# Linear attention into an RWKV channel mix: the attention output handed over by DMA transposes instead of TensorE transposes

## Chip, cores, metric

One core of one Trainium2 chip. The metric is the device time of one execution in microseconds (us). Kernels that are compared were run in turn on the same chip, in several rounds. A run over 1.5% above the fastest of the same kernel counts as slow, and ratios use fast runs alone.

## The reference

Eight batches, 8 heads, 576 tokens, head width 64. Linear attention makes features of q and k (exp of a projection, with its largest magnitude taken off, and exp of the negative), and its output, 576 x 512 per batch, is the input of a channel mix:

```python
proj = x @ w_phi; proj = proj - max(abs(proj)); phi = concat(exp(proj), exp(-proj))
kv = phi(k).T @ v;  z = sum(phi(k));  attn = (phi(q) @ kv) / (phi(q) @ z + 1e-6)
x = attn, heads side by side                       # (8, 576, 512)
xk = mu_k * x + (1 - mu_k) * x_prev                # x_prev: the token before, 0 for the first
xr = mu_r * x + (1 - mu_r) * x_prev
k = relu(xk @ w_k);  v = (k * k) @ w_v;  r = sigmoid(xr @ w_r)
out = r * v
```

## The kernel before

Work goes by pairs of heads, 32 in all (4 per batch). A token is p*9 + s, and the nine values of s are called slots. Attention leaves `x_sc` with tokens on the partitions; the channel mix needs `xs` with features on the partitions. That hand-over is what the change touches. Every instruction group is an `op` with an engine and a planned duration; a long list, `ORDER`, gives the order in which they are emitted, and each engine is given its own in that order.

```python
def rd():                      # VectorE: normalise, out of PSUM
    s["rd"] = small.tile([128, 2, 5], FP, name="rden")
    ...
    nc.vector.tensor_tensor(s["x"]..., ndv[:, :, :, 0:64], s["rd"].to_broadcast(...), op=ALU.mult)

def xt():                      # TensorE: five 128x128 transposes into PSUM
    ps = motile(("mo", "x" + N), "ps_x")
    ...
    for G in range(5):
        nc.tensor.transpose(px[:, G * 128:128 + G * 128],
                            s["x"][:, 2 * G:2 * G + 2, :].rearrange("p h d -> p (h d)"), ident)

def xe():                      # VectorE: four copies PSUM -> xs
    nc.vector.tensor_copy(xs[:, a, 128:640]..., s["px"][:, 0:512]...)
    nc.vector.tensor_copy(xs[:, a, 1:64], s["px"][:, 448:511])       # the slot shifted by one token
    for hh in range(2):
        r = slice(64 * hh, 64 * hh + 64)
        nc.vector.tensor_copy(xs[r, a, 64:128], s["px"][r, 512 + 64 * hh:576 + 64 * hh])

def df():                      # VectorE: x - x_prev
    nc.vector.tensor_tensor(s["d"], xs[:, a, 64:64 + S], xs[:, a, 0:S], op=ALU.subtract)
# then mix(0), mix(1): xk and xr, and h, r, v: the products of the channel mix
```

SyncE's queue issues the output stores (72) and, for batches 2 to 7, one large DMA transpose of q and k each. GpSimd issues the loads of q, k and v, which cast from float32 to bf16.

## Time and profile before

| | before |
|---|---|
| median of the runs | 319.1 us (318.1 to 319.9) |
| TensorE busy / VectorE busy | 283.8 / 251.9 us of a span of 317.5 |
| mean granted TensorE clock | 0.988 |
| VectorE's wait for the transposes of the hand-over | 3.3 us in all |

In profile lines PE is TensorE (PEld its weight loads), DVE VectorE, ACT ScalarE, POOL GpSimd, and a q after a name is that engine's queue; a bracket at a line's end is the engine's idle time before it and what ended it. Busy time is the union of an engine's instructions; the span less that is its idle time (33.7 us on TensorE). The clock is the share of full speed that TensorE was granted.

### The profile page before, as it was taken

The page shows a single profiled execution, that of the slowest core. Times are in us where ns is not written, and L with a number is a line of the kernel's source. Part 1 is how long each engine was busy: PE and PEld are TensorE (multiplying, and loading weights), DVE is VectorE, ACT ScalarE, POOL GpSimd, SP SyncE. Part 2 cuts the span into 40 slices and gives each one's busy share as a digit, 9 for nine tenths or more (in the row PEclk, how much of TensorE's full clock was granted, in tenths as well). Part 3 has the DMA queues.
Part 4 walks back from the last instruction along what each step waited for, and adds up shares of the span by engine and source line. Part 5 has one row for each costly group of instructions (what it writes and reads, how often), then busy time and mean ns, then how long its engine had stood idle before and what let it go on. Part 6 is the DMA issues. An engine that isn't in the chain of part 4 may idle for free.

```text
span 317.5 us, 9126 instructions
## 1 busy us (share of the span) xinstructions
PE 283.8 (89%) x3830; PEld 164.1 (52%) x3830; DVE 251.9 (79%) x466; ACT 216.6 (68%) x318; POOL 145.0 (46%) x248
## 2 busy tenths in 40 slices
PE   1676786988999998999999999999999999999993
PEld 1464464545555654555555654555555655554541
DVE  4656999889989899998987997998887987683021
ACT  2468797667768875787688865779769578733610
POOL 8636311575375465455344632465624504603710
PEclk9999979899999999999999999999999999999999
DMA  8999996087399699574039930367052022114134
GB/s 149 203 209 205 209 162 70 0 129 134 74 186 208 126 168 232 100 139 88 0 68 154 238 53 18 55 145 144 2 125 46 2 46 60 30 39 95 34 68 99
DMA packets 49769, 34.25 MB, mean 108 GB/s; under 512 B 30656, under 2 KB 44352, under 8 KB 49728
## 3 DMA queue, kind: packets, MB, share of 16 engines
q0 software_dynamic: 14624, 16.48, 32.3%
q1 hardware_dynamic: 34960, 16.89, 26.2%
q8 instruction: 30, 0.49, 0.6%
q10 hardware_dynamic: 144, 0.29, 0.3%
q14 instruction: 11, 0.09, 0.1%
HBM read 33.62 MB, written 9.44 MB: 136 GB/s over the span
## 4 chain that ended last, share of the span: by engine, by line
PE 67%; DVE 21%; issue 3%; ACT 3%; DMA 2%; POOL 2%; SPq 0%; DVEq 0%; ACTq 0%
PE ps_v L747 15%; PE ps_h L714 15%; PE ps_r L733 7%; PE ps_nd L607 4%; DVE nm L514 4%; PE ps_kv L588 3%; DVE nm L519 3%; PE ps_x L631 3%; DVE xk L652 2%; PE ps_k L502 2%; PE ps_k L552 2%; DVE x_sc L621 2%; PE ps_ve L832 2%; PE ps_q L502 2%; PE ps_qT L560 2%
## 5 line engine op out<-in xcount | busy, mean ns | idle before, releaser
L725 POOL TENSOR_TENSOR kk<-krelu 128x512 bf16<-128x512 bf16 x64 | 67.0, 1058 | 60.1 <-ACT krelu L720 59.9
L529 ACT ACTIVATE k<-ps_k 128x1024 bf16<-128x1024 f32 x64 | 62.8, 1032 | 9.0 <-PE ps_k L552 8.7
L573 ACT ACTIVATE q<-ps_qT 128x1024 bf16<-128x1024 f32 x64 | 62.7, 1031 | 7.2 <-PE ps_qT L566 7.1
L714 PE MATMUL ps_h<-xk,wk_bf 128*128 128x512 bf16 x256 | 63.6, 381 | 1.2 <-DVE mT L547 0.6
L720 ACT ACTIVATE krelu<-ps_h 128x512 bf16<-128x512 f32 x64 | 38.5, 603 | 34.6 <-PE ps_h L714 28.3
L747 PE MATMUL ps_v<-wv_bf,kk 128*128 128x512 bf16 x256 | 59.7, 379 | 0.0
L514 DVE TENSOR_REDUCE nm<-ps_k 128x8 f32<-128x1024 f32 x32 | 39.0, 1220 | 5.1 <-PE ps_k L502 4.7
L519 DVE TENSOR_REDUCE nm<-ps_q 128x8 f32<-128x1024 f32 x32 | 38.9, 1218 | 3.1 <-PE ps_q L502 2.9
L753 DVE SCALAR_TENSOR_TENSOR ob<-rt,ps_v 128x512 f32<-128x512 bf16 x32 | 21.9, 685 | 22.3 <-PE ps_v L747 20.1
L747 PEld LDWEIGHTS <-kk 128*128 128x128 bf16 x256 | 23.9, 98 | 26.3 <-issue 0.7
L714 PEld LDWEIGHTS <-wk_bf 128*128 128x128 bf16 x256 | 23.2, 98 | 27.1 <-issue 3.5
L538 POOL CAST mhl<-nm 128x16 bf16<-128x16 f32 x32 | 7.4, 230 | 64.0 <-DVE nm L514 58.2
L733 PE MATMUL ps_r<-wr_bf,xr 128*128 128x512 bf16 x128 | 32.6, 380 | 0.1
L652 DVE SCALAR_TENSOR_TENSOR xk<-diff,mu_k_t,xs 128x576 bf16<-128x576 bf16 x32 | 30.4, 951 | 0.4
L739 ACT ACTIVATE rt<-ps_r 128x512 bf16<-128x512 f32 x32 | 19.2, 604 | 15.9 <-PE ps_r L733 15.9
L652 DVE SCALAR_TENSOR_TENSOR xr<-diff,mu_r_t,xs 128x576 bf16<-128x576 bf16 x32 | 28.9, 903 | 0.1
L621 DVE TENSOR_TENSOR x_sc<-ps_nd,rden 128x640 bf16<-128x640 f32 x32 | 26.4, 825 | 1.1
L502 PEld LDWEIGHTS <-qkT 64*128 64x128 bf16 x512 | 17.7, 97 | 13.3 <-issue 10.2
L607 PEld LDWEIGHTS <-q 128*128 128x128 bf16 x512 | 20.6, 101 | 6.2 <-issue 2.0
L607 PE MATMUL ps_nd<-kv,q 128*128 128x65 bf16 x512 | 22.7, 198 | 0.9 <-DVE qkT L298 0.7
L588 PE MATMUL ps_kv<-v,k 64*128 64x65 bf16 x1024 | 22.5, 192 | 0.6 <-DVE x_sc L621 0.2
L523 POOL COPY v<-vt 128x576 bf16<-128x576 bf16 x32 | 22.9, 737 | 0.0
(82 smaller groups left out, 433.3 us busy)
## 6 DMA issues: line engine op xcount, KB each, us to landing
out_dram<-ob SPq DMA_DIRECT2D x72, 128.0 KB, 2.4
nat<-in_k_dram POOLq DMA_DIRECT2D x6, 576.0 KB, 10.9
nat<-in_q_dram POOLq DMA_DIRECT2D x6, 576.0 KB, 9.7
vt<-in_v_dram POOLq DMA_DIRECT2D x6, 576.0 KB, 9.8
wk_bf<-in_moe_w_k_dram POOLq DMA_DIRECT2D x1, 1024.0 KB, 12.4
wv_bf<-in_moe_w_v_dram POOLq DMA_DIRECT2D x1, 1024.0 KB, 10.0
nat<-in_k_dram POOLq DMA_DIRECT2D x3, 288.0 KB, 8.5
nat<-in_q_dram POOLq DMA_DIRECT2D x3, 288.0 KB, 8.7
```

Source lines behind the costliest of these rows:

```text
L514: nc.vector.tensor_reduce(s["nm"][:, 0, :], s["k"].rearrange("p a (g f) -> p (a g) f", f=128), axis=AX.X, op=ALU.max, apply_absolute_value ...
L519: nc.vector.tensor_reduce(s["nm"][:, 1, :], s["q"].rearrange("p a (g f) -> p (a g) f", f=128), axis=AX.X, op=ALU.max, apply_absolute_value ...
L529: nc.scalar.activation(s[f"k{pn}"], s["k"].rearrange("p a (g f) -> p (a g) f", f=128), AF.Exp, scale=(1.0 if pn == 0 else -1.0))
L573: nc.scalar.activation(t.rearrange("f h (c p) -> f c h p", c=8), s["qT"].rearrange("f a (g h p) -> f (a g) h p", g=4, h=2), AF.Exp, scale= ...
L607: nc.tensor.matmul(ps[:, bk, o * 65:(o + 1) * 65], lhsT=s[f"q{pn}"][:, h, G * 128:(G + 1) * 128], rhs=s["kv"][:, h, pn, :], start=(o == 0 ...
L621: nc.vector.tensor_tensor(s["x"].rearrange("p (b s) d -> p b s d", b=2), ndv[:, :, :, 0:64], s["rd"].to_broadcast([128, 2, 5, 64]), op=ALU ...
L652: nc.vector.scalar_tensor_tensor(out=t[:, a, (b % 2) * S:(b % 2 + 1) * S], in0=s["d"], scalar=mu[:, a:a + 1], in1=xs[:, a, 0:S], op0=ALU.m ...
L714: nc.tensor.matmul(ps, lhsT=wk_bf[:, c, fc * 128:(fc + 1) * 128], rhs=xkt[bp][:, c, m0:m0 + 512], start=(c == 0), stop=(c == NDC - 1))
L720: nc.scalar.activation(s["kr", fc], s[fc], AF.Relu)
L725: nc.gpsimd.tensor_tensor(s["kk"][:, fc, :], s["kr", fc], s["kr", fc], op=ALU.mult)
L733: nc.tensor.matmul(ps, lhsT=xrt[bp][:, c, m0 + ci * 128:m0 + (ci + 1) * 128], rhs=wr_bf[:, c, :], start=(c == 0), stop=(c == NDC - 1))
L747: nc.tensor.matmul(ps, lhsT=s["kk"][:, fc, ci * 128:(ci + 1) * 128], rhs=wv_bf[:, fc, :], start=(fc == 0), stop=(fc == NFC - 1))
```

## The change

The intent: TensorE and VectorE are the two full engines, so take the transposes off the first and the copies out of PSUM (the memory where TensorE leaves its products) off the second, and let the DMA write `xs` directly. Side parts: the q0 tail is computed per head (so that both heads' tails land in the same rows), the factor 0.5 on w_v goes into relu as a scale of 0.5**0.5, the output slots are stored in another sequence, the large transpose is cut in two, the load of w_phi goes to ScalarE's queue, and `ORDER` was searched anew for all this. The core of the diff (the order and small lines cut):

```diff
+            x2 = s["x"].rearrange("p h d -> p (h d)")
+            for o, r, c0, c1 in ((64, 128, 0, 256), (320, 64, 512, 640), (384, 128, 256, 512)):
+                nb = (c1 - c0) // 128
+                nc.sync.dma_start_transpose(out=xs[:, a, o:o + nb * r].rearrange("p (g t) -> p g t", g=nb),
+                                            in_=x2[0:r, c0:c1])
+        def xu():
+            nc.vector.tensor_copy(xs[:, a, 1:64], xs[:, a, 576:639])
         def df():
-            nc.vector.tensor_tensor(s["d"], xs[:, a, 64:64 + S], xs[:, a, 0:S], op=ALU.subtract)
+            nc.vector.tensor_tensor(s["d"][:, 0:320], xs[:, a, 320:640], xs[:, a, 0:320], op=ALU.subtract)
+            nc.vector.tensor_tensor(s["d"][:, 320:576], xs[:, a, 64:320], xs[:, a, 320:576], op=ALU.subtract)
...
-            for pn in range(2):
-                nc.tensor.matmul(ps[:, 1, 195:325]..., lhsT=(tqp, tqn)[pn][b][:, a, :], rhs=s["kv"][:, :, pn, :], ...)
+            for h in range(2):
+                for pn in range(2):
+                    nc.tensor.matmul(ps[:, 1, 195 + 65 * h:260 + 65 * h],
+                                     lhsT=(tqp, tqn)[pn][b][:, a, 64 * h:64 * h + 128], ...)
...
-        op("xt" + N, "PE", 0.38, ...)
-        op("xe" + N, "DVE", 0.97, ...)
+        op("xz" + N, "SP", 1.0, ("xt", n), xz, ["rd" + N], ...)
+        op("xz" + N + ".d", "DMA", 2.2, ("xt", n), None, ["xz" + N], rel=[("x", n)])
+        op("xu" + N, "DVE", 0.1, ("xe", n), xu, ["xz" + N + ".d"])
...
-                nc.scalar.activation(s["kr", fc], s[fc], AF.Relu)
+                nc.scalar.activation(s["kr", fc], s[fc], AF.Relu, scale=HALF)
```

The planned costs in the `op` lines: 1.0 us on SyncE's queue for all three transposes of a pair, and 2.2 us to land.

## The prediction

> **What bounds the kernel now.** I read the page first (busy shares, the slices, the chain that ended last), then busy time by stretch, then the timeline of one attention pair's hand-over to the channel mix, then the groups, then the queue of SyncE.
>
> The busy shares and the row of slices:
>
> ```profile
> PE 283.8 (89%) x3830; PEld 164.1 (52%) x3830; DVE 251.9 (79%) x466; ACT 216.6 (68%) x318; POOL 145.0 (46%) x248
> ...
> PE   1676786988999998999999999999999999999993
> ...
> PE 67%; DVE 21%; issue 3%; ACT 3%; DMA 2%; POOL 2%; SPq 0%; DVEq 0%; ACTq 0%
> ```
>
> A slice is 317.5/40 = 7.9 us. TensorE is nearly full from the ninth slice (64 us) to the end; before that it is not. The last line is the chain that ended last: two thirds TensorE, a fifth VectorE, nothing else of weight. The same by stretch (us, then busy us of PE, PEld, DVE, ACT, POOL, clock, DMA share, GB/s):
>
> ```profile
> 0.00:64.00 64.00, 43.53 (x711) 29.93 (x713) 49.57 (x102) 42.31 (x65) 29.55 (x69) 0.95 0.89 150
> 64.00:280.00 216.00, 208.09 (x2952) 119.06 (x2947) 190.86 (x346) 163.66 (x237) 105.25 (x170) 1.00 0.55 102
> 280.00:317.50 37.50, 32.19 (x181) 15.12 (x177) 11.44 (x20) 10.58 (x18) 10.23 (x10) 0.99 0.33 71
> ```
>
> From 64 to 280 us TensorE is busy 208.1 of 216 us (96%) and VectorE 190.9 (88%): TensorE bounds, VectorE is close behind, and with both this full each sometimes makes the other wait. Before 64 us loads (DMA share 0.89) and VectorE hold TensorE to 68%. After 280 us only channel-mix products are left and no pair. So what the change saves must be saved in the first two stretches.
>
> One hand-over in the timeline (start us, duration us):
>
> ```profile
> 159.43 0.45 PE L631 MATMUL ps_x<-ident,x_sc 128*128 128x128 bf16 x5
> 159.67 1.45 PEld L747 LDWEIGHTS <-kk 128*128 128x128 bf16 x8
> 159.72 1.89 PE L747 MATMUL ps_v<-wv_bf,kk 128*128 128x512 bf16 x8
> 159.92 0.42 DVE L637 COPY xs<-ps_x 128x512 bf16<-128x512 bf16 x1 [1.15 <-PE ps_x L631]
> 160.26 0.18 DVE L639 COPY xs<-ps_x 128x63 bf16<-128x63 bf16 x1
> 160.36 0.38 DVE L642 COPY xs<-ps_x 64x64 bf16<-64x64 bf16 x2
> 160.78 0.46 DVE L646 TENSOR_TENSOR diff<-xs 128x576 bf16<-128x576 bf16 x1
> 161.27 0.82 DVE L652 SCALAR_TENSOR_TENSOR xk<-diff,mu_k_t,xs 128x576 bf16<-128x576 bf16 x1
> ```
>
> Durations overlap on an engine, so I count from start to start: the five transposes hold TensorE 159.72-159.43 = 0.29 us (not the 0.45 shown), the four copies hold VectorE 160.78-159.92 = 0.86 us, the difference 0.49 us.
>
> **What the Trainium skill says.**
> - "VectorE: DVE Perf Modes", section "The three transpose paths", gives 390 ns for a 128x128 transpose on TensorE and 1309 ns through the DMA. Here TensorE's transpose takes 219 ns alone and 0.29/5 = 0.06 us in a run, so a DMA transpose is no faster thing; its merit is only that it occupies neither bound engine and needs no copy out of PSUM.
> - "DMA: Bandwidth & Descriptors", section "DMA Transpose (X-bar)", demands a 2-byte type, a partition count that is a multiple of 16, SBUF as destination, and one stream of transposes at a time. The new transposes are bf16 on 128 or 64 partitions, and all go out on SyncE's queue beside the old ones: allowed.
> - The same page, section "Anatomy of one DMA", puts a fixed cost of about 2 us on a DMA for completion. It is written for GpSimd's path; the trace shows 2.4 us to landing for an output store issued from SyncE, which agrees in size.
> - "VectorE: DVE Perf Modes", section "Rules for kernel authors", says bf16 from SBUF to SBUF runs tensor_tensor at twice the plain rate. The trace agrees: the difference takes 458 ns (median), while the scaled add of the same 576 elements takes 819.
>
> **The change, part by part.**
>
> Transposes off TensorE: 32 pairs x 0.29 = -9.3 us of TensorE's queue. The chain gives line 631 3% of the span, 0.03 x 317.5 = 9.5 us, the same size.
>
> Copies off VectorE: 32 x 0.86 = -27.5 us. What comes back: the shifted slot is copied alone (63 columns; the like copy above starts 0.10 us before its follower) and the difference is cut into 320 and 256 columns. The cut adds one fixed share. I take it from the two scaled adds, which start 0.73 us apart elsewhere in this trace, less 576 columns at 0.96 per ns (the skill's VectorE clock, "Trainium Kernel Development and Optimization", NeuronCore Architecture) = 0.60: 0.13 us. So +32 x 0.23 = +7.4 us.
>
> Half into relu: the 1.22 us scaling of wv_bf goes, and relu gets a constant scale, free on the same instruction: -1.2 us of VectorE once.
>
> q0 tails per head: two products of 130 columns become four of 65. In the timeline 16 products of 65 columns run 0.51 us from start to start, 0.032 each, so four take 0.13 us, against 0.11 for the two: +0.02 x 32 = +0.6 us. Four more small fills at the start (88 ns for a like one): +0.4 us of VectorE, under the loads.
>
> Sum: TensorE 283.8-9.3+0.6 = about 275 us busy; VectorE 251.9-27.5+7.4-1.2+0.4 = about 231 us.
>
> DMA and SyncE: a pair issues three DMA transposes, 4.5 blocks of 128x128. The old transpose carries 36 blocks, 5.50 us of issue and 9.0 us to landing, so 0.153 us a block, and 3.5 us from the end of issue to landing. 4.5 blocks give 0.7 us by size; a small store takes 0.6 us to issue, so three instructions could take 1.8. I take 1.3 us of issue, 32 x 1.3 = 42 us in all, on a queue that mostly waits. To landing: 1.3 + 2.4 to 3.5 = 4 to 5 us after x_sc is ready. Before, TensorE and VectorE did it in 0.29 + 0.86 plus a short wait. So a pair gets 2 to 4 us more latency. That is hidden where the order puts other VectorE work between.
>
> I added up, from the new order and this trace's start-to-start times, the VectorE work between each pair's normalisation and its first reader of the landed data: 1.9 to 10.4 us, median about 4.9. With 4.5 us needed, 13 pairs of 32 have less, and are short by 14 us in all. But VectorE has waits of its own in that time (it will be idle about a quarter of the span), and a stall of VectorE reaches TensorE only in part: I charge a quarter, about 3.5 us.
>
> The gain on the path: TensorE -9.3 +0.6 = -8.7 us; VectorE is freed by 21 us, and its 21% of the chain suggests some 0.21 x 21 = 4.4 us; then +3.5 for late landings. -8.7 -4.4 +3.5 = -9.6 us. 319.8 - 9.6 = 310.2, and I round down to **309.5 us**, as the order was searched again for the lighter engines.
>
> **The rivals.**
> 1. *The wait for the landing takes the place of the copies.* Loads fill the DMA in the first 50 us, and an input load of 576 KB takes about 10 us to land; transposes share its engines. If landing takes 6.5 us, the same sum of shortfalls is 54 us, VectorE (in order) holds back the reductions behind it, and a quarter of that is 13 us: 319 to 322 us. For it: the old transposes landed in 7.3 to 11.6 us. Against: they are eight times as large, and DMA is only half busy after 64 us.
> 2. *SyncE's queue blocks.* Its waits in order are long; who waited for whom on it (total us, times, longest us):
>
> ```profile
> SPq L760 <- DVE ob L753: 124.9, 16, 18.6
> SPq L305 <- DMA nat<-in_k_dram: 56.0, 2, 34.5
> ```
>
> A transpose behind such a wait would be late. Against: I compared the new order, and no pair's transposes stand behind a store whose result VectorE makes after that pair's x_sc; the large transposes are cut in two (2.8 us each), and few stand in between. If it did happen for a third of the pairs: 316 us.
> 3. *Nothing much moves*, because the freed engine time is not where the end is set (the first 64 us are held by loads; the last 37 us contain no pair): 314 to 317 us. Against: 28 or so of the 32 hand-overs lie in the full stretch.
> 4. *More than the removed work comes back.* TensorE is idle 8 us between 64 and 280 and 20 us before; a VectorE with 21 us less to do could close a third of that: 300 to 303 us.
>
> **Range and chances.** Centre 309.5. Rival 4 sets the low end, 301; rivals 1 to 3 the high end, 318. Two per cent is 6.4 us, so faster means under 313.4. My central sum clears that by 4 us; rivals 1, 2 and 3 together have about three chances in ten. Faster 0.71, within 0.23, slower 0.06.
>
> **What would show it.** Right: the group of ps_x gone; TensorE near 275 and VectorE near 231 us; three transposes of x_sc per pair, 1 to 1.8 us of issue and 2.4 to 4 us to landing; VectorE's waits for the DMA of xs under 15 us in total; the stretch from 64 us on still full of TensorE. Wrong: if VectorE waits for xs by more than 30 us and TensorE has holes there, rival 1; if SyncE's transposes wait at the queue's head behind stores, rival 2; if TensorE's busy time falls by 9 but its idle time grows by as much without waits on xs, the order found elsewhere gave it back.

## More of the kernel before

The profile's own lines stand in the prediction. One more is needed later, from who waited for whom (total us, times, longest):

```profile
DVE xs L637 <- PE ps_x L631: 3.3, 5, 1.2
```

VectorE's first copy (line 637) waited five times for TensorE's transposes, never long.

## The result and the profile after

The changed kernel takes 354.5 us (median of 4 runs, 351.1 to 357.3) against 319.1 us. The ratio is 1.103, with a 95% interval of 1.097 to 1.108: slower by 10%. (A ratio is the mean time of one kernel's fast runs over that of the other's of the same rounds, so not quite the ratio of the quoted medians.) The profiled run was one of the slower, 357.3 us with a span of 355.5; a second profile is reported below and reads the same.

The page's busy shares, the slices, and the chain that ended last:

```profile
PE 283.7 (80%) x3690; PEld 163.3 (46%) x3734; DVE 230.7 (65%) x405; ACT 215.7 (61%) x318; POOL 143.0 (40%) x248
...
PE   1877486869836999956993999899729998987994
...
PEclk9998668999969999997897899999968999999999
...
PE 40%; DVE 20%; DMA 16%; SPq 12%; issue 4%; POOL 4%; ACT 2%; DVEq 0%; ACTq 0%; POOLq 0%
DMA xs<-x_sc 13%; SPq L646 9%; PE ps_v L761 8%; PE ps_h L728 8%; PE ps_r L747 4%; PE ps_kv L599 3%; PE ps_nd L618 2%; DVE xk L661 2%; DVE nm L525 2%; SPq L313 2%; DVE nm L530 2%; DVE xr L661 2%; DVE x_sc L634 2%; PE ps_he L815 2%; DVE ob L767 2%
```

VectorE's busy time fell by 21 us to 230.7, as planned. TensorE's did not fall, although nine microseconds of transposes are gone, and its row now has holes all along. The clock's row has holes at nearly the same places. The chain that ended last now runs through the new transposes: 13% of the span in their landing and 9% in their issue (line 646), 22% of 355.5 = 78 us where there was nothing. TensorE's idle time is 355.5 - 283.7 = 71.8 us, 38 more than before, which is the whole difference of the spans (355.5 - 317.5 = 38). (44 of TensorE's 3734 matmuls are missing from this profile; the second profile has all, with 285.9 us busy of a span of 354.3.)

Who waited for whom, and the instructions on the tile x_sc with the time from issue to landing of its transposes (durations in ns, minimum/median/maximum):

```profile
DVE xs L650 <- DMA xs<-x_sc: 44.5, 15, 9.9
```

```profile
L646 SPq DMA_TRANSPOSE xs<-x_sc x96: 1167/1240/3963, 30.2 to 322.3; - x96
...
DMA to landing us min/median/max: 2.3/3.3/10.4
```

VectorE's first reader of the landed data waits 44.5 us in all, in 15 of the 32 pairs, where it had waited 3.3. Each transpose, be it two blocks of 128x128 or half a block, holds SyncE's queue for 1.2 us, so three hold it for about 3.7; from the first issue of a pair to the end of its third the median over the pairs is 4.0 us.

What such a wait looks like, from the timeline around pair 23:

```profile
243.80 10.18 SPq L313 DMA_TRANSPOSE qkT<-nat  x2
...
246.86 0.82 DVE L634 TENSOR_TENSOR x_sc<-ps_nd,rden 128x640 bf16<-128x640 f32 x1
...
254.08 1.18 SPq L774 DMA_DIRECT2D out_dram<-ob  x2
...
255.35 10.92 SPq L646 DMA_TRANSPOSE xs<-x_sc  x6
...
261.36 0.18 DVE L650 COPY xs<-xs 128x63 bf16<-128x63 bf16 x1 [9.87 <-DMA xs<-x_sc]
...
262.57 0.61 PE L571 MATMUL ps_qT<-qkT,wph 64*128 64x512 bf16 x2 [6.54 <-DVE x_sc L634]
...
266.47 1.91 PE L728 MATMUL ps_h<-xk,wk_bf 128*128 128x512 bf16 x4 [0.22 <-issue]
```

x_sc is ready at 247.7 us. SyncE is then in two large transposes and two stores, and issues this pair's first transpose only at 255.35. The data is there at 261.3, and VectorE has stood still for 9.87 us. Behind the reader stands the next pair's normalisation (line 634): its products were done at 250.5 us, but VectorE takes its instructions in order and starts it at 261.45. TensorE waits for it and idles 6.54 us. And its clock drops: the stretches by ten microseconds show 0.50 from 260 to 270 us (after the columns of busy time of PE, PEld, DVE, ACT, POOL: clock, DMA share, GB/s):

```profile
250.00:260.00 10.00, 5.98 (x115) 3.40 (x113) 1.09 (x3) 4.59 (x6) 0.11 (x1) 0.98 0.83 130
260.00:270.00 10.00, 5.58 (x44) 3.15 (x45) 5.35 (x10) 2.49 (x4) 1.03 (x1) 0.50 0.11 21
```

Four products of 512 columns take 1.91 us there, from the first start to the last end, and 1.02 to 1.04 in the kernel before between 250 and 280 us. The Trainium skill, "TensorE: Matmul & The Clock Gate", section "Why this matters for your kernels", warns of the half clock after idle gaps of more than some 3 us between bursts of matmuls; the gap of 6.54 us with 0.50 after it agrees, and so do the other three gaps over 4 us after 64 us. Not every drop has such a gap: in the kernel before the clock was 0.50 from 40.4 to 43.8 us, after a stretch of 3.4 us with TensorE busy for 2.05 and no gap over 0.6. After 64 us the kernel before was never at half clock, the changed one for 30.7 us. This is why TensorE's busy time did not fall: the removed 9 us came back as the same products at a lower clock (0.928 on average, against 0.988).

### The profile page after: what moved, and what is told of

Its sections match the earlier page's. It is cut to its first block, busy times and chain, and to the rows that moved or that the text cites.

```text
span 355.5 us, 8980 instructions
## 1 busy us (share of the span) xinstructions
PE 283.7 (80%) x3690; PEld 163.3 (46%) x3734; DVE 230.7 (65%) x405; ACT 215.7 (61%) x318; POOL 143.0 (40%) x248
## 4 chain that ended last, share of the span: by engine, by line
PE 40%; DVE 20%; DMA 16%; SPq 12%; issue 4%; POOL 4%; ACT 2%; DVEq 0%; ACTq 0%; POOLq 0%
DMA xs<-x_sc 13%; SPq L646 9%; PE ps_v L761 8%; PE ps_h L728 8%; PE ps_r L747 4%; PE ps_kv L599 3%; PE ps_nd L618 2%; DVE xk L661 2%; DVE nm L525 2%; SPq L313 2%; DVE nm L530 2%; DVE xr L661 2%; DVE x_sc L634 2%; PE ps_he L815 2%; DVE ob L767 2%
## 5 line engine op out<-in xcount | busy, mean ns | idle before, releaser
L728 PE MATMUL ps_h<-xk,wk_bf 128*128 128x512 bf16 x236 | 64.7, 395 | 11.6 <-DVE ob L767 9.7
L584 ACT ACTIVATE q<-ps_qT 128x1024 bf16<-128x1024 f32 x64 | 62.8, 1031 | 17.4 <-PE ps_qT L577 16.9
L549 POOL CAST mhl<-nm 128x16 bf16<-128x16 f32 x32 | 6.4, 200 | 96.3 <-DVE nm L525 84.8
L650 DVE COPY xs<-xs 128x63 bf16<-128x63 bf16 x32 | 10.5, 332 | 44.5 <-DMA xs<-x_sc 44.5
L661 DVE SCALAR_TENSOR_TENSOR xk<-diff,mu_k_t,xs 128x576 bf16<-128x576 bf16 x32 | 27.4, 855 | 0.3
L661 DVE SCALAR_TENSOR_TENSOR xr<-diff,mu_r_t,xs 128x576 bf16<-128x576 bf16 x32 | 26.6, 835 | 0.0
L618 PEld LDWEIGHTS <-q 128*128 128x128 bf16 x512 | 21.5, 102 | 8.0 <-issue 3.5
L599 PE MATMUL ps_kv<-v,k 64*128 64x65 bf16 x1024 | 24.0, 198 | 1.4 <-ACT q L584 0.9
L513 PEld LDWEIGHTS <-qkT 64*128 64x128 bf16 x512 | 19.9, 101 | 10.8 <-issue 7.9
L599 PEld LDWEIGHTS <-k 64*128 64x128 bf16 x1024 | 21.5, 99 | 6.4 <-issue 4.1
## 6 DMA issues: line engine op xcount, KB each, us to landing
nat<-in_k_dram POOLq DMA_DIRECT2D x6, 576.0 KB, 10.9
```

The costliest lines, as they stand in the source:

```text
L584: nc.scalar.activation(t.rearrange("f h (c p) -> f c h p", c=8), s["qT"].rearrange("f a (g h p) -> f (a g) h p", g=4, h=2), AF.Exp, scale= ...
L599: nc.tensor.matmul(ps[:, hh, pn * 65:(pn + 1) * 65], lhsT=s[f"k{pn}"][r, c, :], rhs=vb[r, a, 2 * g + par, :], start=(pn == 0 and c == 0), ...
L661: nc.vector.scalar_tensor_tensor(out=t[:, a, (b % 2) * S:(b % 2 + 1) * S], in0=s["d"], scalar=mu[:, a:a + 1], in1=xs[:, a, 0:S], op0=ALU.m ...
L728: nc.tensor.matmul(ps, lhsT=wk_bf[:, c, fc * 128:(fc + 1) * 128], rhs=xkt[bp][:, c, m0:m0 + 512], start=(c == 0), stop=(c == NDC - 1))
```

## The experiments

Theory 1: the three small transposes cost a fixed issue time each, so the data lands too late, VectorE waits in order, and TensorE behind it. Theory 2: the landing beside other transfers is what is late. Theory 3: the side parts or the new order are to blame. Twelve runs were made. The result of each is its ratio to the kernel before of the same rounds. Differences in us between kernels are taken between the medians of their fast runs, 351.9 us for the changed one.

### The side parts alone, in the old order

```diff
# the kernel before, with:
+ tails per head, relu with scale=HALF, fills of the tail tiles
- op("wvs", "DVE", 1.2, ...)           # the scaling of wv
-   two copies of 64 partitions of the tail out of PSUM
+   one copy: nc.vector.tensor_copy(xs[:, a, 64:128], s["px"][:, 512:576])
```

> The kernel before, with its own order and its TensorE transposes, but with the side parts of the change: q0 tails per head, half put into relu, the scaling of wv gone (and, since both tails now stand in the same rows, one copy of the tail out of PSUM instead of two). Theory 1 (the slow issue of the three small DMA transposes is the cause): the side parts cost nothing, 311 to 320 us, a little under before because VectorE loses 32 copies of 0.19 us. Theory 3 (the side parts cost): over 325 us.

Measured: 314.0 us (312.0 to 314.8), ratio 0.983 (0.979 to 0.988), correct. These side parts are not the cause; they gain 1.7%. (The new sequence of slots, the cut of the large transpose and the queue of w_phi are not in this run; they are in the hand-over for nothing, below.) VectorE's busy time fell to 242.8 us, and with both tails in the same rows one copy does for two. This is the fastest correct kernel, under both the kernel before and the changed one, though by less than 2% under before.

### One transpose in place of three

The slots are laid out as 1 3 5 7 | shifted, 0 | 2 4 6 8, so that the five blocks are adjacent; the half of the tail block that holds nothing of use becomes the place of the shifted slot.

```diff
-            for o, r, c0, c1 in ((64, 128, 0, 256), (320, 64, 512, 640), (384, 128, 256, 512)):
-                ...
+            nc.sync.dma_start_transpose(out=xs[:, a, :].rearrange("p (g t) -> p g t", g=5), in_=x2)   # 640 columns
```

> The changed kernel, same order, but one DMA transpose of five blocks per pair in place of three of 2, 0.5 and 2 blocks (the output slots are laid out anew so that the five blocks are adjacent; VectorE does one small subtract and one tiny fill more per pair). Theory 1 (about 1.24 us of issue per transpose, whatever its size): issue per pair falls from about 4.0 to between 1.3 and 1.8 us, VectorE's waits for xs fall from 44 to about 20 us (what is left is late landing beside loads and the queue behind large transposes), time 325 to 335 us. Theory 2 (the landing beside loads is the cause, not the issue): waits stay near 40 us and the time at 345 to 355. If the issue goes by blocks (0.8 us each), it stays near 4 us.

Measured: 334.3 us (332.0 to 340.5), ratio 1.047, correct. The tile's instructions, and VectorE's wait:

```profile
L639 SPq DMA_TRANSPOSE xs<-x_sc x32: 1200/1209/1786, 29.7 to 303.6; - x32
...
DMA to landing us min/median/max: 2.6/2.8/12.0
...
DVE xs L642 <- DMA xs<-x_sc: 23.5, 6, 7.7
```

Five blocks in one instruction hold the queue as long as half a block did: 1.2 us. VectorE's wait for xs falls from 44.5 to 23.5 us, and 18 us of the loss of 33 go. Theory 1 holds, for about half of the loss. The rest is in six pairs whose single transpose went out within 2 us of x_sc and landed late, each with a load in flight.

### Four transposes in place of three

```diff
-((64, 128, 0, 256), (320, ...), (384, ...))
+((64, 128, 0, 128), (192, 128, 128, 256), (320, ...), (384, ...))
```

> The changed kernel with the first of the three DMA transposes cut in two: four per pair, the same bytes. Theory 1: 1.24 us more of issue per pair (about 5.2), VectorE's waits for xs rise from 44 to 65 or more, time 370 to 385 us. Theory 2 (landing, bytes): within 1% of the changed kernel, 350 to 358 us.

Measured: 382.8 us (377.6 to 385.3), ratio 1.196, correct. Again 1.2 us each, and VectorE waits 65.3 us for xs:

```profile
L646 SPq DMA_TRANSPOSE xs<-x_sc x128: 1107/1231/2619, 30.8 to 348.1; - x128
...
DVE xs L650 <- DMA xs<-x_sc: 65.3, 21, 8.5
```

The bytes are the same; one more instruction per pair cost some 30 us. This is the opposite step to the one before, and it goes the other way; per instruction it cost more than the two instructions taken away there gave back (18 us).

### TensorE's transposes in the new order

```diff
# the changed kernel, with
- xz: three DMA transposes;  xu: one copy
+ xz: five TensorE transposes into PSUM, at the place of xu;  xu: four copies out of PSUM
```

> The changed kernel in its own new order, but with TensorE's transposes and the copies out of PSUM put back next to the place where the order has the first reader of the landed data. Theory 1: the DMA path is the cause, so this stands near before, 315 to 328 us. Theory 3 (the new order or the side parts are the cause): over 340 us.

Measured: 348.1 us, ratio 1.094, correct. By the words of its expectation that spoke for theory 3. But the experiment had a fault of mine: with no place in the order for TensorE's transposes, I put them directly ahead of the copies, and VectorE now waited for TensorE's queue instead of the DMA (24.8 us, 20 times, against 3.3 in the kernel before). It says how badly a hand-over fits that was placed without the search, and nothing sure of the order. A hand-over for nothing tells them apart better.

### The hand-over for nothing, in the new order

```diff
-            (the three transposes)
+            pass          # xs holds a constant; the result is wrong on purpose
```

> The changed kernel, same order, without any transposes between x_sc and xs (wrong result on purpose; xs holds a constant from the start, its readers run as before): the hand-over for nothing. If the DMA path (issue and landing) is the whole cause of the loss, this should be under the kernel before, 300 to 312 us. If the new order or the side parts have a cost of their own, as the version with TensorE's transposes in the new order (348 us) may say, it stays over 325 us.

Measured: 317.8 us, ratio 0.993. This one too had a fault: the fill of xs ran on VectorE ahead of the first copies, two instructions of 2.19 us, and put the first copy out of PSUM at 14.32 us instead of 9.00. So it was done again with small fills on GpSimd:

> The free hand-over again (no transposes between x_sc and xs, wrong result on purpose), without the fault of the first try: there the two whole-tile fills of xs ran on VectorE ahead of the first copies and put the first pair 5 us later. Here GpSimd fills each part of xs at the place of the transposes of the first eight pairs. If the DMA path is the whole cause of the loss: 306 to 313 us. If the new order has a cost of its own: it stays at 317 us or more.

Measured: 313.1 us (312.1 to 314.8), ratio 0.981 (0.974 to 0.989). So the order and the side parts do not make the kernel slower than before, theory 3 falls as the cause of the loss, and the whole difference, some 37 to 39 us between fast runs, is the DMA path (issue, queue and landing together). It shows a second thing: even if the hand-over cost nothing at all, this order would have gained 1.9% over before, no more than the side parts gain in the old order with TensorE's transposes kept (1.7%). In this order, then, taking the transposes and the copies off the two engines brought nothing beyond that. The traces show one thing that may be why: in the first 64 us TensorE's clock was 0.84 here, as in the changed kernel, and 0.95 in the kernel before and with the side parts alone. No run tests it.

### No input loads after the second batch

Pairs whose transpose went out soon still waited for its landing. Are loads the reason? I matched every transpose with its landing in the trace of the one-transpose kernel: 13 with a load in flight took 7.7 us from issue to landing (median, up to 12.0), 19 without took 2.6 (up to 4.4). In the changed kernel the two medians are 7.1 and 2.4. So the loads of batches 2 to 7 were left out: these batches reuse the data of the first two, and all other work stays. Their outputs are wrong, which doesn't matter for the times.

```diff
+                if b >= 2:
+                    nat[b] = nat[b - 2]     # and vt likewise
+                    return
```

> One transpose per pair, and no input loads after the second batch (wrong result on purpose: the later batches reuse the first two batches' data, all other work is the same). If the rest of the loss of the one-transpose version is transposes landing late beside loads (7.7 us median with a load in flight, 2.6 without), landing falls to 2.6 us throughout, VectorE's waits for xs fall from 23 to under 8 us, time 308 to 320 us. Rival (the order itself): 326 us or more, whatever the landing does.

Measured, one transpose and no later loads: 311.7 us (311.5 to 313.0), ratio 0.977. The wait for xs is nearly gone:

```profile
DVE xs L648 <- DMA xs<-x_sc: 1.9, 2, 1.0
```

> The changed kernel with its three transposes, and no input loads after the second batch (wrong result on purpose). The issue of 3.7 us and more per pair stays, late landing goes: VectorE's waits for xs fall from 44 to about 25 us, time 328 to 340 us. If issue alone were the cause: no change, 350 us or more.

Measured, three transposes and no later loads: 327.8 us (325.1 to 328.7), ratio 1.025. The wait is 17.4 us, lower than the 25 expected.

> Control: the kernel before without input loads after the second batch (wrong result on purpose). Nothing there reads a small DMA transpose, so loads cost it little: 312 to 320 us.

Measured, the kernel before without later loads: 317.8 us (317.4 to 318.8), ratio 0.995. The loads as such cost the old kernel next to nothing; they cost the new one because its transposes land late beside them. Taking loads away is worth 24 us with three transposes and 22 with one; taking two transposes away is worth 18 us with loads and 16 without. Both causes are shown, and each is worth nearly the same with the other as without it: 351.9 - 311.7 = 40 us together.

### The changed kernel once more

> The changed kernel unchanged, for a second profile and for times of the same chip as the free hand-over: 350 to 358 us, VectorE's waits for xs 40 to 48 us.

Measured: 354.1 us (347.8 to 357.1), ratio 1.095, wait for xs 42.0 us, clock 0.923. The profile repeats.

### The waits against the spans

The profiles of the new order side by side (without the two runs that had a fault), times in us; span and wait are of the same profiled run:

| transposes per pair | loads | span | VectorE waits for xs | span less wait | clock | state of the profiled run |
|---|---|---|---|---|---|---|
| 4 | all | 381.3 | 65.3 | 316.0 | 0.906 | fast |
| 3 (the change) | all | 355.5 | 44.5 | 311.0 | 0.928 | slow |
| 3, again | all | 354.3 | 42.0 | 312.3 | 0.923 | slow |
| 3 | first two batches | 325.5 | 17.4 | 308.1 | 0.973 | fast |
| 1 | all | 338.6 | 23.5 | 315.1 | 0.917 | slow |
| 1 | first two batches | 309.7 | 1.9 | 307.8 | 0.957 | fast |
| 0 (free, second try) | all | 310.5 | 0 | 310.5 | 0.958 | fast |

The wait runs from 0 to 65 us; what is left of the span lies between 308 and 316. About as much as VectorE waited for the landing came out in the time. Between fast profiles alone, counted from the hand-over for nothing: 65.3 us of wait made 70.8 us, and 17.4 us made 15.0. The states differ, so a few microseconds in a row are not to be read; the sixty are.

### Can the order be mended?

Since late landing beside loads can be foreseen, the order for one transpose was searched again, in a rough model of the five engines. For a control, the side parts with TensorE's transposes were put through the same search.

```diff
-ORDER = (the changed kernel's)
+ORDER = (searched: readers of xs on average later; 1.25 us of issue, 7.5 to 9.5 us beside a load)
```

> One transpose per pair, in an order searched again (in a rough model of the engines with this study's costs in it: 1.25 us of issue, 1.4 to 2 us from the end of issue to landing, 7.5 to 9.5 us where an input load is in flight), so that the readers of the landed data stand later on VectorE. Theory: the time is about 310 us plus VectorE's waits for xs; with these under 5 us the kernel is at 305 to 315 us, under the kernel before. Rival (late landing cannot be scheduled around): waits of 15 us or more and over 322 us.

Measured: 336.2 us (333.9 to 344.1), ratio 1.048, correct; VectorE still waits 19.1 us for xs. It is no faster than one transpose in the changed kernel's order (1.047). That the readers stand later is true of the model; in the traces VectorE works 6.5 us on average between a pair's normalisation and its reader in both orders.

> Control for the search: TensorE's transposes and the side parts, in an order searched in the same way for as long. If the one-transpose version owes its time to the new search and not to the DMA, this is as fast: 305 to 313 us. If the search does not do anything for it, it stays at the 314 us of the side parts in the old order, or over it.

Measured: 332.1 us (331.3 to 332.8), ratio 1.039, correct. The control is 18 us worse than the same kernel in the old order (314.0), so my search makes poorer orders than the kernel's own, and the try says nothing on whether a good one exists. That stays open.

## Why the prediction was wrong

It said 309.5 us, 301 to 318, and 71 in 100 for faster. Two steps failed: the latency of a hand-over, taken as 4.5 us for every pair, was 6.5 us (median over the pairs, from x_sc to the last landing, up to 15.7), and of VectorE's wait for it not a quarter but all reached the time. Step by step:

- **TensorE about 275, VectorE about 231 us busy.** VectorE: right, 230.7. TensorE: about right as work, as the free hand-over (276.7) and the one without loads and with one transpose (276.3) show; in the changed kernel it was 283.7, because idle gaps brought the clock down. No step of the prediction had the clock in it.
- **"I take 1.3 us of issue"** per pair. Failed. It was a choice between 0.7 us by size and 1.8 by three instructions, and both were too low: 1.2 us per instruction whatever its size, 3.7 per pair and 4.0 with what delays it. I had scaled the large transpose, 0.153 us a block; that line does not go through small ones. The same mistake stands in the planned 1.0 us of the `op` line.
- **Landing 2.4 to 3.5 us after the end of issue.** Too long without a load (1.1 to 1.4 us after the end, 2.3 to 2.6 from the start), and too short beside one, where a transpose took 7.1 us from its start in the median, up to 10.4. In a pair that met neither load nor queue the two wrong terms cancelled, by luck: 3.7 of issue and 1.1 of landing make 4.8 us, near the 4.5 forecast. The loads and the queue made the 6.5. I had named the loads as rival 1, with the right sign, and put it aside with two arguments that both failed: that these transposes are small (the size did not matter) and that the DMA is only half busy after 64 us (the loads come one after another, and 36 of the 96 transposes met one).
- **"I charge a quarter"** of VectorE's shortfall. Failed. My own list of slack (sum of shortfalls 14 us at 4.5 us of latency, 54 at 6.5) had the size of it and no more: the measured wait of 44.5 us lies between the two, for latencies that ran from 4.9 to 15.7 us; without loads, at 5.9 us in the median, it was 17.4. But all of it reached the time, not a quarter: those 17.4 us, too, put the span 15.0 us over that of the hand-over for nothing. VectorE executes in order, and behind the waiting reader stands work that TensorE waits for, as in pair 23; the idle gap then costs a second time, by the half clock (283.7 us of TensorE's busy time, against 276.7 with the hand-over for nothing).
- **The gain of 8.7 + 4.4 us.** Too high. With the hand-over for nothing the kernel stands 6 us under before. The reason for that gap was not tested; the lower clock in the first 64 us (0.84 against 0.95) may be part of it.
- **Rival 2, SyncE's queue.** Partly. Between x_sc and the first issue the pairs lost 35.8 us in all, most of it in a few pairs behind large transposes and stores, as in pair 23 (7.7 us). SyncE was issuing in nearly all of that time and not waiting for a store's data, so the argument against this rival was right as far as it went. With one transpose it fell to 10.9 us: much of the blocking was thus by the small transposes themselves.

So the mechanism was rival 1 and in part rival 2, with an issue cost three times what I gave it. The end of rival 1, 319 to 322 us, was itself too low by some 30 us, for the quarter's sake. One small estimate came out well: the cut of the difference, put at 0.13 us, cost 0.15 (medians of 324 + 284 against 458 ns).

## What to carry to other kernels

A DMA instruction in place of engine work has a price per instruction on the queue that issues it; before many small ones are put on a path, measure one small one, and do not scale a large one down. Landing time must be taken with the other transfers that will be in flight, and the reader's place in an in-order engine set by the late landing, since all that stands behind the reader waits too. And an idle gap of a few microseconds on TensorE can cost more than itself through the clock, so a change that removes work from it may leave its busy time as it was. What a change can gain at most can itself be run: here the hand-over for nothing gained no more than the side parts alone.

## What the Trainium skill lacked or had wrong

- "DMA: Bandwidth & Descriptors", section "DMA Transpose (X-bar)", has no cost of issuing a transpose; the page's only figures for it stand in a comparison for a newer chip and are for other shapes. Here one from SyncE, SBUF to SBUF, holds its queue for 1.2 us for half a block to five blocks of 128x128, 2.7 to 2.9 us for 18 and 5.5 us for 36 (at their shortest; one of 18 took up to 8.0).
- The same page, section "Issuing engines are not separate DMA queues", calls the time to initiate a DMA usually small beside the DMA itself. For these small transposes issue took 1.2 us, and landing came 1.1 to 1.4 us after its end.
- No page gives the landing time of a small DMA transpose beside loads: for one of five blocks 2.6 us from issue to landing alone, 7.7 us median and up to 12.0 with a casting input load in flight.
- "VectorE: DVE Perf Modes", section "The three transpose paths", gives 1309 ns for a 128x128 transpose by DMA. For a reader that waits, five blocks took 2.6 us alone and the smaller ones 2.2 us at the least, so a cost per block misleads.
